# An mLSTM cell and a feed-forward on one core: cell steps visited in pairs, masks issued ahead

## Chip, core and metric

One core of a Trainium2 chip runs the whole kernel. The metric is the device time of one execution in microseconds (us), the median of the runs shown. Engines: PE is TensorE (PEld its weight loads), DVE VectorE, ACT ScalarE, POOL GpSimd, SP the engine that issues nearly all DMAs here.

## The reference, cut to what matters

Per batch row and head an mLSTM recurrence over 768 tokens; the result, laid out as 3072 tokens of 320, goes through a feed-forward of width 2048 with a leaky ReLU.

```python
# q, k, v, o_gate: (4, 8, 768, 40); i_gate, f_gate: (4, 8, 768)
for t in range(S):
    m_new = max(f[t] + m, i[t])
    f_stab, i_stab = exp(f[t] + m - m_new), exp(i[t] - m_new)
    m = m_new
    C = f_stab * C + i_stab * outer(v[t], k[t])          # 40 x 40 per head
    n = f_stab * n + i_stab * k[t]
    y[t] = sigmoid(o[t]) * (C @ q[t]) / max(abs(n . q[t]), 1)
x = y.transpose(0, 2, 1, 3).reshape(3072, 320)
h = x @ w_in                                             # 320 x 2048
out = maximum(0.01 * h, h) @ w_out                       # 2048 x 320
```

## The kernel before

The 768 tokens are cut into six chunks of 128 (c = 0 to 5). A **step** s is one chunk of one batch row, s = 4c + b, with all eight heads; there are 24. A step is computed in two halves of 64 tokens (u = 0, 1): scores inside a half, and a carried state of 40 x 42 per head that is advanced at each half's end.

The feed-forward runs one chunk behind the cell. In stage c, for c = 2 to 5, TensorE does the feed-forward of chunk c - 1 in 32 units, `ff_units(c - 1)`: units 0 to 15 are eight `pair`s of hidden tiles (`first` with three of the five contraction slots, `second` with the other two and the leaky ReLU on ScalarE), units 16 to 31 are the sixteen `part`s of the output, four for each batch row. Between units, in an order written out by hand, stand the cell's **visits** for chunk c, listed by `cell_units(c)`:

- `u_parts(s)`: scores and the two halves' state increments, into two PSUM banks `sd0`, `sd1` (64x64 tiles of TensorE, L595 and L600); then DVE multiplies the scores by the decays `w` into `qn` (L605) and adds the first increment to the state (`state_add`, L577).
- `u_mix(s)`: the output product, `pT` (L676); POOL advances the state (`state_next`, L573); DVE turns `pT` into blocks `hb` (L683), forms the denominators and the gated value in `xb` (L687), POOL divides (L690), DVE adds the second increment, which frees `sd1`, and turns `xb` back into `x` (L694); SP stores it to DRAM (`x_dr`, L697).
- `u_gates(c + 1)`: the gates of the next chunk turned to token order, `tg` (L312, L317), and copied out by DVE (L322, L324).

Stage 1 has `u_plain` in place of `u_mix`, and `u_x`, which transposes on TensorE. There the weights' conversion from 64-bit words still runs on DVE and ACT, dripped between the units (`now`).

What a step needs ahead of its visit is issued by `ahead(s)` (L814): the exponentials `prep_exp` (eight on ACT, L439, over `w` in place), `prep_kq` (two transposes and two multiplications on DVE, L486, L492), the loads of k, q and the decays `ea` for step s + 2, POOL's `state_next(s, 0)` and `prep_vu` (L459), and `prep_mask(s + 1)`, which adds the causal mask to the next step's `w` on POOL (L431). In stages 2 to 5 `ahead(s + 1)` follows `u_parts(s)`; in stage 1 it follows `u_plain(s)`, but for the last step. The exponentials lie in `lazy` and are issued three a unit from then on, ahead of the unit's own work; what is left is flushed in `u_parts`.

`gather_x` (L711) brings the stored `x` of a step into `xT`, the feed-forward's input, once unit 15 of the stage is through. After a mix, `load_late` loads the step-after-next's output gate, and `feed(s + 4)` loads k, v and `w` of the same row in the next chunk. The buffers that matter: `kqT`, `ea`, `vu`, `x` and `rb` (k, q, o as blocks) twice, `w` four times, `hb`, `xb` and `xT` once; PSUM has a pool `psc` of four banks for the cell and a pool `psf` of four for the feed-forward (`ph`, `po`). The orders on PE, DVE, ACT and POOL are those of the program text; SP's order is chosen by the scheduler.

Where the visits stand is one line (L957); with nine visits and 32 units they follow units 2, 5, 7, 10, 13, 15, 18, 21 and 23, one at a time:

```python
upto = sum(p <= i for p in place) if c == 1 else min(n_c, (i + 1) * n_c // (n_ff - 8))
```

Of the kernel before, what the change touches and what calls it, by code (L numbers as in the profile page):

```python
# [18 lines left out]
def kernel(  # L19
# [27 lines left out]
    B, H, S, D = q.shape  # L47
    P = 128
    BH = B * H
    NB = S // P  # L50
    NS = B * NB
# [86 lines left out]
    def subs(s):  # L138

        for u in range(2):  # L140
            yield u, ts(u, SL), slice(SL * (1 - u), SL * (1 - u) + D)
# [78 lines left out]
    def narrow_weights(n):  # L220

        if not wide:
            return
        raw, dst = raws.pop(n)
        words = raw.bitcast(U32).rearrange("p (c two) -> p c two", two=2)
        lo, hi = words[:, :, 0], words[:, :, 1]
        d = dst.bitcast(U32)
        low, top = lo.bitcast(F32), hi.bitcast(F32)  # L230
        nc.scalar.activation(dst, top, AF.Abs)
        yield
        nc.vector.tensor_scalar(
            dst, dst, scalar1=2.0**-15, scalar2=122879.9921875, op0=ALU.max, op1=ALU.min,
        )
        yield
        nc.vector.tensor_scalar(
            d, d, scalar1=0x07FFFFFF, scalar2=3, op0=ALU.bitwise_and, op1=ALU.logical_shift_left,
        )
        yield  # L240
        nc.vector.scalar_tensor_tensor(d, in0=hi, scalar=0xC0000000, in1=d, op0=ALU.bitwise_and, op1=ALU.bitwise_or)  # L241
        yield
        nc.vector.tensor_scalar(hi, d, scalar1=0xFF800000, scalar2=None, op0=ALU.bitwise_and)  # L243
        yield
        nc.vector.scalar_tensor_tensor(low, in0=lo, scalar=2.0**-52, in1=top, op0=ALU.mult, op1=ALU.mult)  # L245
        yield
        nc.vector.tensor_tensor(dst, dst, low, op=ALU.add)  # L247
# [108 lines left out]
    def natural(s, i):  # L356

        t = rb_t[s % NR][:, i]
        return t[:, : H * D].rearrange("p (h d) -> p h d", d=D)
# [67 lines left out]
                )  # L427

    def prep_mask(s):
        w = st[s]["w"]  # L430
        nc.gpsimd.tensor_tensor(w, w, cm2.unsqueeze(1).to_broadcast([P, H, SL]), op=ALU.add)  # L431

    def prep_exp(s):

        c, b = divmod(s, B)
        w = st[s]["w"]
        for h in range(H):
            bh = b * H + h
            yield nc.scalar.activation(w[:, h, :], w[:, h, :], AF.Exp, bias=gT[c][:, 0, bh : bh + 1], scale=1.0)  # L439
# [23 lines left out]
    def prep_qs(s):  # L463

        c, b = divmod(s, B)
        d = st[s]
        d["qs"] = wk.tile([P, Dm], F32, name="y")[:].rearrange("p (h d) -> p h d", d=D)
        nc.gpsimd.tensor_tensor(
            d["qs"], natural(s, 1), gT[c][:, 2, ts(b, H)].unsqueeze(2).to_broadcast([P, H, D]), op=ALU.mult,
        )  # L470
# [10 lines left out]
    def prep_kq(s):  # L481

        d = st[s]
        d["kqT"] = wk.tile([P, 2, PR * P], F32, name="kqT")
        for i in range(2):
            nc.vector.transpose(  # L486
                d["kqT"][:, i].rearrange("p (h t n) -> p h n t", n=TS, t=QW),
                raw_blocks(s, i, QW).rearrange("p (h n) d -> p h n d", n=TS),
            )
        for r in range(2):  # L490
            rows = ts(r, SL)
            nc.vector.tensor_tensor(  # L492
                mixed(s)[rows, 1 - r], d["kqT"][rows, 1].rearrange("p (h t) -> p h t", t=SL), d["ea"][rows], op=ALU.mult,
            )
# [10 lines left out]
    def u_split(s):  # L505

        d = st[s]
        d["kqT"] = wk.tile([P, 2, PR * P], F32, name="kqT")
        src = (d["k"], natural(s, 1))
        bank = [psc.tile([P, H, SL], F32, name=f"tk{r}", tag="c") for r in range(2)]  # L510
        for h in range(H):
            for i in range(2):
                for u, toks, rows in subs(s):
                    out_rows = rows if i == 0 else slice(SL * u, SL * u + D)
                    nc.tensor.matmul(
                        bank[u][out_rows, h, :], lhsT=src[i][toks, h, :D], rhs=ident[toks, toks], start=True, stop=True,
                    )
        for i in range(2):
            for u, toks, rows in subs(s):
                out_rows = rows if i == 0 else slice(SL * u, SL * u + D)  # L520
                nc.scalar.copy(d["kqT"][rows, i].rearrange("p (h t) -> p h t", t=SL), bank[u][out_rows])
# [275 lines left out]
        gates_T(c, bus.pop(c)[0])  # L797

    def cell_units(c):
        units = [(fn, c * B + n) for n in range(B) for fn in (u_parts, u_mix if c > 1 else u_plain)]  # L800
        if c + 1 < NB:
            units.insert(2 * B - 2, (u_gates, c + 1))
        if c == 1:
            units += [(u_x, s) for s in range(B, 2 * B)]
        return units

    lazy = {}

    def run(steps, n=None):

        for _ in range(H if n is None else n):
            next(steps, None)

    def ahead(s):  # L814

        if s < NS:
            if s < 2 * B:
                u_split(s)
            lazy[s] = prep_exp(s)
            if s < 2 * B:  # L820
                prep_qs(s)
            else:
                prep_kq(s)
            if s + NR < NS:
                load_late(s + NR, 0)
                load_late(s + NR, 1)
                if s + NR >= 2 * B:
                    spread_q(s + NR)
            state_next(s, 0)
            prep_vu(s)  # L830
            if s + 1 < NS:
                prep_mask(s + 1)

    def feed(s):
        load(s)
        spread(s)
# [78 lines left out]
    with tc.manual_schedule(engines={E.PE, E.DVE, E.Activation, E.Pool}):  # L915
        ffs = first_chunk()
        for s in (B, B + 1):
            feed(s)
            for i in range(1, 3):
                load_late(s, i)  # L920
            if s == B:
                load_weights(3)
        for n in range(3):
            load_weights(QN + n)
        for s in (B + 2, B + 3):
            feed(s)


        ffs = ffs[2:]
        fetch = {4: (3, 4), 8: (5, 6), 15: (7,)}  # L930
        place = (2, 5, 7, 10, 12, 15, 16, 18, 21, 22, 24, 26, 28)
        now = (None for n in range(2, QN + NF // 2) for _ in narrow_weights(n))
        for c in range(1, NB + 1):
            if c > 1:
                ffs = ff_units(c - 1)
            cells = cell_units(c) if c < NB else []
            n_ff, n_c = len(ffs), len(cells)
            done = fed = 0
            waiting = []
            for i in range(n_ff):  # L940
                if c == 1:
                    run(now, 2 if i < 10 else 3 if i < 14 else 4)
                    for n in fetch.get(i, ()):
                        load_weights(QN + n)
                    if i == 0:
                        prep_mask(B)
                        ahead(B)
                        load_fi(3)
                for steps in lazy.values():
                    run(steps, 3)  # L950
                ffs[i]()
                if c + 1 < NB:
                    if i == (1 if c == 1 else 0):
                        gates(c + 1)
                    if i == (3 if c == 1 else 2):
                        gates_exp(c + 1)
                upto = sum(p <= i for p in place) if c == 1 else min(n_c, (i + 1) * n_c // (n_ff - 8))  # L957
                while done < upto:
                    fn, s = cells[done]
                    fn(s)  # L960
                    done += 1
                    if fn is u_mix:
                        waiting.append(s)
                    if fn in ((u_mix, u_plain) if s < 2 * B - 1 else (u_parts,)):
                        ahead(s + 1)
                if i >= n_ff // 2 - 1:
                    for s in waiting:
                        gather_x(s)
                    waiting.clear()
                while fed < done:  # L970
                    fn, s = cells[fed]
                    fed += 1
                    if fn in (u_mix, u_plain):
                        load_late(s + NR, 2)
                        if s + NL < NS:
                            feed(s + NL)
# [31 lines left out]
```

## Time and profile before

| | |
|---|---|
| runs | 533.64, 534.17, 535.91 us; median 534.17 |
| profiled execution | 533.48 us, its span 531.7, mean granted clock 0.98 |
| PE, PEld busy | 517.3, 334.5 us of the span |
| DVE, ACT, POOL busy | 241.1, 168.0, 111.1 us |
| chunk boundaries on PE | 139.6, 219.6, 299.7, 379.8, 459.2 us |

A row of the profile says how often an instruction ran and how long one took; L12 is line 12 of the kernel. A busy PE is no sign of work at full speed[...]. A matmul in float32 leaves two records. "Idle before" is the engine's idle time ahead of an instruction, with what ended it; "issue" means that nothing in the profile did. A DMA's row on SP is its issue.

### The profile page before, as it was taken

The page shows a single profiled execution, that of the slowest core. Times are in us where ns is not written, and L with a number is a line of the kernel's source. Part 1 is how long each engine was busy: PE and PEld are TensorE (multiplying, and loading weights), DVE is VectorE, ACT ScalarE, POOL GpSimd, SP SyncE. Part 2 cuts the span into 40 slices and gives each one's busy share as a digit, 9 for nine tenths or more (in the row PEclk, how much of TensorE's full clock was granted, in tenths as well). Part 3 has the DMA queues.
Part 4 walks back from the last instruction along what each step waited for, and adds up shares of the span by engine and source line. Part 5 has one row for each costly group of instructions (what it writes and reads, how often), then busy time and mean ns, then how long its engine had stood idle before and what let it go on. Part 6 is the DMA issues. An engine that isn't in the chain of part 4 may idle for free.

```text
span 531.7 us, 11350 instructions
## 1 busy us (share of the span) xinstructions
PE 517.3 (97%) x4501; PEld 334.5 (63%) x4501; DVE 241.1 (45%) x431; ACT 168.0 (32%) x458; POOL 111.1 (21%) x145
## 2 busy tenths in 40 slices
PE   7879989999999999999999999999999999999997
PEld 7767878667545577545577555577555577544675
DVE  4788998999055526055616055614054432000000
ACT  4566767515434311134311134311134300122100
POOL 4245254153022223022223012323011100000000
PEclk9768999999999999999999999999999999999999
DMA  9977677878745647555547555546531221000000
GB/s 116 161 205 161 146 185 183 185 143 175 157 92 114 125 121 162 120 119 112 125 132 146 131 114 102 130 136 151 123 73 39 66 71 43 32 1 0 14 12 25
DMA packets 165284, 59.13 MB, mean 111 GB/s; under 512 B 128816, under 2 KB 156016, under 8 KB 165232
## 3 DMA queue, kind: packets, MB, share of 16 engines
q1 hardware_dynamic: 164848, 58.28, 50.2%
q8 instruction: 35, 0.57, 0.4%
q10 hardware_dynamic: 384, 0.13, 0.1%
q14 instruction: 17, 0.14, 0.1%
HBM read 51.68 MB, written 6.70 MB: 110 GB/s over the span
## 4 chain that ended last, share of the span: by engine, by line
PE 81%; DVE 7%; SPq 6%; DMA 2%; ACT 2%; issue 1%; POOL 1%; ACTq 0%; DVEq 0%; POOLq 0%
PE po L775 36%; PE ph L740 36%; PE pT L676 3%; SPq L213 3%; PE sd L595 3%; SPq L338 2%; DVE raw L245 1%; SPq L352 1%; PE sd L600 1%; DVE qn L605 1%; DVE w_out L247 1%; DMA rb<-in_q_dram 1%; DVE w_out L241 1%; DVE raw L243 1%; DMA raw<-in_moe_w_in_dram 1%
## 5 line engine op out<-in xcount | busy, mean ns | idle before, releaser
L740 PE MATMUL ph<-xT,w_in 64*128 64x512 f32 (+1 forms) x1120 | 217.3, 538 | 0.6 <-ACT acts L748 0.6
L775 PE MATMUL po<-w_out,acts 128*128 128x320 f32 x768 | 213.3, 435 | 0.0
L775 PEld LDWEIGHTS po<-w_out,acts 128*128 128x128 f32 x768 | 143.8, 190 | 59.7 <-issue 1.8
L740 PEld LDWEIGHTS ph<-xT,w_in 64*128 64x128 f32 x1120 | 107.1, 189 | 91.1 <-issue 84.4
L748 ACT ACTIVATE acts<-ph 128x512 f32<-128x512 f32 (+1 forms) x112 | 53.9, 534 | 145.6 <-PE ph L740 145.5
L605 DVE TENSOR_TENSOR qn<-w,sd 64x512 f32<-64x512 f32 x40 | 27.4, 686 | 125.6 <-PE sd L600 90.1
L573 POOL TENSOR_TENSOR S<-S,f 40x336 f32<-40x336 f32 x36 | 30.7, 854 | 187.8 <-PE pT L676 146.8
L439 ACT ACTIVATE w<-w,gT 128x64 f32<-128x64 f32 (+1 forms) x192 | 52.5, 351 | 1.0 <-DVE w L425 1.0
L783 ACT COPY y<-po 128x320 f32<-128x320 f32 x12 | 5.1, 426 | 86.6 <-PE po L775 86.6
L783 ACT COPY hn<-po 128x320 f32<-128x320 f32 x12 | 5.1, 427 | 86.3 <-PE po L775 86.3
L690 POOL TENSOR_TENSOR xb<-xb,den 128x320 f32<-128x320 f32 x16 | 11.7, 729 | 88.9 <-DVE xb L687 88.9
L431 POOL TENSOR_TENSOR w<-w,i 128x512 f32<-128x512 f32 x20 | 26.7, 1333 | 10.2 <-DMA w<-a_dr 10.1
L683 DVE STREAM_TRANSPOSE hb<-pT 128x512 f32<-128x512 f32 x16 | 11.5, 717 | 38.1 <-PE pT L676 38.1
L595 PEld LDWEIGHTS sd<-kqT 40*64 40x64 f32 x640 | 20.3, 135 | 10.8 <-issue 9.3
L595 PE MATMUL sd<-kqT 40*64 40x64 f32 x640 | 23.0, 221 | 0.0
L492 DVE TENSOR_TENSOR qn<-kqT,ea 64x512 f32<-64x512 f32 x32 | 22.4, 701 | 1.1
L676 PEld LDWEIGHTS pT<-qn,S 128*64 128x64 f32 x512 | 16.2, 138 | 10.5 <-issue 6.9
L600 PE MATMUL sd<-S,vu 64*40 64x42 f32 x576 | 20.6, 215 | 0.7 <-POOL vu L459 0.7
L694 DVE STREAM_TRANSPOSE x<-xb 128x512 f32<-128x512 f32 x16 | 17.6, 1102 | 8.0 <-POOL xb L690 8.0
L486 DVE STREAM_TRANSPOSE kqT<-rb 128x512 f32<-128x512 f32 x32 | 20.7, 682 | 0.0
L600 PEld LDWEIGHTS sd<-S,vu 64*40 64x40 f32 x576 | 18.2, 111 | 0.8 <-POOL vu L459 0.8
L577 DVE TENSOR_TENSOR S<-S,sd 40x336 f32<-40x336 f32 x36 | 18.1, 503 | 0.9
(126 smaller groups left out, 369.1 us busy)
## 6 DMA issues: line engine op xcount, KB each, us to landing
w<-a_dr SPq DMA_DIRECT2D x40, 128.0 KB
rb<-in_k_dram SPq DMA_DIRECT2D x64, 80.0 KB
rb<-in_q_dram SPq DMA_DIRECT2D x64, 80.0 KB
rb<-in_o_gate_dram SPq DMA_DIRECT2D x64, 80.0 KB
ea<-a_dr SPq DMA_DIRECT2D x32, 128.0 KB
kn<-in_k_dram SPq DMA_DIRECT2D x24, 160.0 KB
raw<-in_moe_w_out_dram SPq DMA_DIRECT2D x6, 640.0 KB
S<-in_v_dram SPq DMA_DIRECT2D x80, 40.0 KB
```

The lines of the kernel that those rows point to most:

```text
L431: nc.gpsimd.tensor_tensor(w, w, cm2.unsqueeze(1).to_broadcast([P, H, SL]), op=ALU.add)
L439: yield nc.scalar.activation(w[:, h, :], w[:, h, :], AF.Exp, bias=gT[c][:, 0, bh : bh + 1], scale=1.0)
L486: nc.vector.transpose(d["kqT"][:, i].rearrange("p (h t n) -> p h n t", n=TS, t=QW), raw_blocks(s, i, QW).rearrange("p (h n) d -> p h n d", ...
L492: nc.vector.tensor_tensor(mixed(s)[rows, 1 - r], d["kqT"][rows, 1].rearrange("p (h t) -> p h t", t=SL), d["ea"][rows], op=ALU.mult,)
L573: nc.gpsimd.tensor_tensor(new, old, g, op=ALU.mult)
L595: nc.tensor.matmul(bank[1 - u][toks, h, :], lhsT=kqT[rows, 0, ts(h, SL)], rhs=kqT[rows, 1, ts(h, SL)], start=True, stop=True,)
L600: nc.tensor.matmul(dC[u][:, h].rearrange("p k d -> p (k d)"), lhsT=d["ku"][toks, h], rhs=S_v[s % NL][toks, u, h, :, :V1], start=True, stop ...
L605: nc.vector.tensor_tensor(mixed(s)[toks, u], w[toks], bank[1 - u][toks], op=ALU.mult)
L676: nc.tensor.matmul(pT[DP * r : DP * (r + 1), j * P + u * SL : j * P + (u + 1) * SL], lhsT=S[:, u, h, :], rhs=m[:, u, h, :], start=True, st ...
L740: nc.tensor.matmul(ph[r][:, cols], lhsT=w_row(r, slot, j), rhs=xT[DP * r : DP * (r + 1), slot, cols], start=(slot == 0), stop=(slot == KC ...
L748: nc.scalar.activation(acts[:, f, cols], ph[r][:, cols], AF.Prelu, alpha=0.01)
L775: nc.tensor.matmul(po[n][:], lhsT=acts[:, f, ts(n, P)], rhs=w_out[:, f, :], start=(f == 0), stop=(f == NF - 1),)
```

## The change

In stages 2 to 5 the visits of two steps stand together: `u_parts` of both after unit 2, `u_mix` of both after unit 6, `u_parts` of the other two after unit 14, and after unit 19 `u_gates` and their two `u_mix`. `ahead(s + 2)` now follows `u_mix(s)`. The exponentials of a step wait three units before they start. The masks are issued on POOL at unit 0 (steps 2 and 3 of the chunk) and at unit 12 (the first two of the next chunk), and at the end of stage 1 for step 9; `masked` keeps a mask from being added twice. In stage 1 the order of the visits stays, and `ahead(9)` follows `u_plain(7)`.

```diff
     def prep_mask(s):
+        if s in masked:
+            return
+        masked.add(s)
         w = st[s]["w"]
...
     def cell_units(c):
-        units = [(fn, c * B + n) for n in range(B) for fn in (u_parts, u_mix if c > 1 else u_plain)]
+        if c == 1:
+            units = [(fn, c * B + n) for n in range(B) for fn in (u_parts, u_plain)]
+            units.insert(2 * B - 2, (u_gates, c + 1))
+            return units + [(u_x, s) for s in range(B, 2 * B)]
+        units = [(fn, c * B + n + m) for n in range(0, B, 2) for fn in (u_parts, u_mix) for m in range(2)]
         if c + 1 < NB:
             units.insert(2 * B - 2, (u_gates, c + 1))
-        if c == 1:
-            units += [(u_x, s) for s in range(B, 2 * B)]
         return units
...
     def ahead(s):
...
+            if s >= 2 * B:
+                late[s] = 3
             lazy[s] = prep_exp(s)
...
-            if s + 1 < NS:
+            if s + 1 <= 2 * B:
                 prep_mask(s + 1)
...
+        late = {}
+        masks = {0: (2, 3), 12: (4, 5)}
+        pairs = (2, 2, 6, 6, 14, 14, 19, 19, 19)
...
-                for steps in lazy.values():
-                    run(steps, 3)
+                for s, steps in lazy.items():
+                    if s in late and late[s] > 0:
+                        late[s] -= 1
+                    else:
+                        run(steps, 3)
+                for n in masks.get(i, ()) if 1 < c < NB else ():
+                    if c * B + n < NS:
+                        prep_mask(c * B + n)
                 ffs[i]()
...
-                upto = sum(p <= i for p in place) if c == 1 else min(n_c, (i + 1) * n_c // (n_ff - 8))
+                upto = min(n_c, sum(p <= i for p in (place if c == 1 else pairs)))
                 while done < upto:
...
-                    if fn in ((u_mix, u_plain) if s < 2 * B - 1 else (u_parts,)):
+                    if fn is u_plain and s < 2 * B - 1 or fn is u_parts and s == 2 * B - 1:
                         ahead(s + 1)
+                    elif fn is u_mix:
+                        ahead(s + 2)
+                    elif fn is u_plain:
+                        prep_mask(s + 2)
+                        ahead(s + 2)
```

More of the change, by code (lines that the diff above doesn't have):

```diff
@@ L799, in cell_units @@
     def cell_units(c):
-        units = [(fn, c * B + n) for n in range(B) for fn in (u_parts, u_mix if c > 1 else u_plain)]
+        if c == 1:
[3 more added lines that the diff above has]
+        units = [(fn, c * B + n + m) for n in range(0, B, 2) for fn in (u_parts, u_mix) for m in range(2)]
         if c + 1 < NB:
             units.insert(2 * B - 2, (u_gates, c + 1))
-        if c == 1:
-            units += [(u_x, s) for s in range(B, 2 * B)]
         return units
+    masked = set()
     lazy = {}
```

## The prediction

> **What bounds the kernel now.** I read the page first (busy shares, chain), then busy time by chunk, then the timeline of the weight loads around one visit, then the DMA queue's timeline. The page (busy time; the chain by engine):
>
> ```profile
> PE 517.3 (97%) x4501; PEld 334.5 (63%) x4501; DVE 241.1 (45%) x431; ACT 168.0 (32%) x458; POOL 111.1 (21%) x145
> ...
> PE 81%; DVE 7%; SPq 6%; DMA 2%; ACT 2%; issue 1%; POOL 1%; ACTq 0%; DVEq 0%; POOLq 0%
> ```
>
> TensorE bounds it, and where it does not (the first 45 us, and chunk 1, where VectorE converts weights) the change does nothing much. By chunk (start:end, length, busy of each engine; chunk 3, chunk 5, the closing feed-forward):
>
> ```profile
> core 0: us, PE busy (x) PEld busy (x) DVE busy (x) ACT busy (x) POOL busy (x), PEclk, DMA share, GB/s
> 219.60:299.70 80.10, 80.10 (x679) 47.71 (x678) 34.50 (x64) 20.28 (x60) 17.05 (x20) 1.00 0.59 129
> 379.80:459.20 79.40, 79.40 (x609) 47.06 (x608) 26.75 (x48) 17.50 (x48) 7.12 (x9) 1.00 0.24 61
> 459.20:531.70 72.50, 69.30 (x289) 39.65 (x288) 0.00 (x0) 10.81 (x21) 0.00 (x0) 1.00 0.03 12
> ```
>
> In chunks 2 to 5 TensorE is busy without a gap at full clock; no other engine passes 44%. So only TensorE's own time counts there, unless a new wait appears. The chain shows the feed-forward alone, in the last stage:
>
> ```profile
> 459.31 34.53 PE ph L740 x160
> 493.85 34.66 PE po L775 x128
> ```
>
> That is 69.19 us. Chunk 3 does the same 288 records in 80.10, so its four `u_parts`, four `u_mix` and one `u_gates` cost 10.9. What one visit costs, from TensorE's weight loads (start, length, count, idle before):
>
> ```profile
> 225.72 0.19 PEld L740 LDWEIGHTS ph<-xT,w_in 64*128 64x128 f32 x2 [0.24 <-issue]
> 226.67 0.14 PEld L595 LDWEIGHTS sd<-kqT 40*64 40x64 f32 x2 [0.76 <-issue]
> ...
> 227.75 0.30 PEld L740 LDWEIGHTS ph<-xT,w_in 64*128 64x128 f32 x4
> 228.28 0.19 PEld L740 LDWEIGHTS ph<-xT,w_in 64*128 64x128 f32 x2 [0.23 <-issue]
> 228.72 0.19 PEld L740 LDWEIGHTS ph<-xT,w_in 64*128 64x128 f32 x2 [0.24 <-issue]
> ...
> 233.96 1.01 PEld L676 LDWEIGHTS pT<-qn,S 128*64 128x64 f32 x32 [0.76 <-issue]
> ```
>
> Undisturbed, pairs of loads stand 0.43 us apart (0.19 + 0.24). From 225.72 to 228.72 there are four pairs, 1.72 us undisturbed, but 3.00 pass: the visit costs 1.28. Inside a visit the records repeat evenly: the 32 `pT` loads take 1.01, less the last load's 0.14, over 15 steps: 0.058 a step; 16 steps are 0.93. So **0.35 us of each visit is entering and leaving**: the weights of the first matmul behind a switch are not loaded under the matmul before (idle 0.76 instead of 0.24), and the same on the way back.
>
> [...] `ph` runs as 64x128 tiles, `sd` as 64x64, `pT` as 128x64, `po` as 128x128, and a visit shows two switches of some 0.17 us each (0.35/2). [...] Here the last gather's issue ends at 296.46 and the matmul that reads it starts at 299.71 without a wait, so its landing is hidden, by an unknown part of 3.2 us.
>
> **The change, part by part.**
>
> *Joined visits (the gain).* Per chunk 2 to 4, nine visits become four: parts+parts after i=2, mix+mix after i=6, parts+parts after i=14, gates+mix+mix after i=19. Chunk 5: eight become four. Sixteen joins of equal mode (4 per chunk) save two switches each, 16 x 0.35 = 5.6. Three joins of gates to mix still change mode once, so about one switch: 3 x 0.17 = 0.5. Together 6.1. How well a second step follows the first is not in the trace: at best without loss (0)[...]. I take 0.04, as inside `ph` a pair that waits for ScalarE keeps the 0.43 rhythm: 16 x 0.04 = 0.6. **Gain 5.5** (bounds 3.4 to 6.1). No instruction is added; the numbers of matmuls, VectorE, GpSimd and DMA instructions stay, only places change.
>
> *PSUM.* Two `u_parts` hold all four psc banks; `sd1` of each is free only after its own `u_mix`. In the compiled order the two `pT` of the first pair take the two `sd0` banks (free after `state_add` of i=2, VectorE done about 4 us before). In the second pair `tg` takes one `sd0`, `pT` the other, and the last `pT` takes `tg`'s, freed by the L324 copy. In chunk 3 `tg` ended near 269.0 and that copy ended about 269.5; the first `pT` keeps TensorE busy until about 0.95 after `tg`. Cost 0; if VectorE were late there, a few tenths, three times.
>
> *VectorE.* Two mixes and two `ahead` in a row: `hb` to `x` is 155.05 to 158.95, 3.9 us, `prep_kq` 2.7 (149.67 to 152.42), so 13.2 us from i=6. With units of 2.57 (first), 1.72 (second) and 2.15 (`part`) and joined visits of 2.2, i=6 ends at 17.6 us of the chunk and the next parts start at 37.0: done by 32, 5 us to spare. Parts at 6.9 take VectorE 3.8 (4 x 0.69 + 2 x 0.50) after 9.1: 13 before 17.6. Cost 0.
>
> *Masks (POOL).* 1.33 us each (L431), the same number, now at i=0 and i=12. A mask waits for its `w` DMA; behind it on POOL stands `state_next` of the mix at 17.6 us. *Exponentials* start three units later, six a unit at 0.25 to 0.35 us: some 5 us of ScalarE in about 6.5 beside 2 to 3 us of relus; a relu may come 2 us late, and the four psf banks give a pair of 4.3 us. Cost 0. *Chunk 1:* `ahead(9)` comes after `u_plain(7)`, 2.7 us of VectorE at about 130, where it falls idle from 134 to 148. Cost 0, give or take 0.5.
>
> *SP and the chunk's end* (what is late next). A joined mix lets its DMAs out together. The queue before, at a chunk's end (start, length, what):
>
> ```profile
> 260.87 2.01 SPq L382 DMA_DIRECT2D rb<-in_k_dram  x4
> 262.98 1.87 SPq L382 DMA_DIRECT2D rb<-in_q_dram  x4
> 264.95 1.10 SPq L405 DMA_DIRECT2D ea<-a_dr  x2
> ...
> 290.52 1.56 SPq L697 DMA_DIRECT2D x_dr<-x  x4
> ...
> 293.90 2.56 SPq L711 DMA_DIRECT2D xT<-x_dr  x4
> ```
>
> After: `pT` of the third step ends near 51.4 us of the chunk, `x` is ready 4.0 later, 55.4. Ahead of the last gathers in the compiled order stand, twice, x_dr, k, q, ea: 2 x (1.56 + 2.01 + 1.87 + 1.10 + 0.4 of gaps) = 13.9, then eight gathers at 0.67: 5.4. Issued at 74.7, landed perhaps 1.5 later, 76.2. The next chunk starts at 78.3 to 78.7. Slack about 2 us; cost 0. What follows on SP (o, kn, v and w of two steps, 22 issues, 12.5 us) ends near 9 us of the next chunk, so the i=0 masks are done before 13: POOL's `state_next` has 4 us to spare.
>
> **Sum:** 533.48 (profiled; span 531.7) - 5.5 = 528.0. The median of the runs is 0.69 above the profiled one: **528.7**.
>
> **Rivals.** (1) *Joins nearly not free*[...]; 16 x 0.18 + 0.5 = 3.4, and a chunk-end wait of 0.5 us four times takes 2: gain 1.4, 532.8, no change. For it: each join brings new waits; against: `ph` pairs with waits lose nothing. (2) **Slower: the gathers come late.** The 36 issues from `x_dr` to the last gather are back to back; k and q bring 80 KB in 0.49 us, about 163 GB/s, as much as the busiest of the page's 40 slices in chunks 2 to 5 moved (162), and one such group took 3.17 instead of 2.0 (283.45). Past the 2 us of slack each microsecond counts four times: 1.4 us late cancels the gain, 2.1 us makes it slower by over 0.5%. At 3.5 late: 528.7 + 14 = 542.7. Against it: now it also ends close (296.46 for 299.71) and holds. (3) *The change doesn't do what it says*: a bank, mask or exponential makes TensorE wait inside a joined visit, 3 us (VectorE's chain after `pT`) at up to eight mixes, 552; the compiled bank order speaks against it.
>
> **Chances.** Forecast (gain over 2.7, the bound of 0.5%, about what a measurement of this kernel tells from no change) 0.73; rival 1 and small chunk-end waits, within 0.5%, 0.14; rival 2 0.10 and rival 3 0.03, slower, 0.13. Low end: gain 6.1 plus 0.5 of chunk 1 and 0.6 for the runs' spread, 527.0. High end: rival 1's 532.8 and a few tenths of gathers late, 534.0; beyond lie rivals 2 and 3. The forecast's own range is 527.0 to 531.5.
>
> **What would show it.** Right: chunks 2 to 4 of about 78.7 us, chunk 5 78.2, `pT` in runs of 64 records over about 2.0 us, no idle TensorE; `ph` of the next chunk not released by a DMA. Wrong: an idle of TensorE ahead of `pT` ended by VectorE (bank), ahead of `ph` ended by xT's DMA (rival 2), relus held by exponentials, or a gap of 0.2 us between two `sd` or `pT` runs (rival 1).

## The result, and the profile after

The changed kernel takes **528.66 us** in the median of six runs (528.14 to 530.43); the kernel before took 534.22 on the same chip (533.18 to 535.91). The ratio is 0.9896, 95% interval 0.9876 to 0.9915: **faster by 1.0%**, where 528.7 was forecast. The profiled execution took 528.25 us, its span 526.4.

The page of the changed kernel, busy time and the chain by engine:

```profile
PE 513.2 (97%) x4501; PEld 336.3 (64%) x4501; DVE 240.3 (46%) x431; ACT 168.1 (32%) x458; POOL 113.0 (21%) x145
...
PE 83%; SPq 6%; DVE 4%; DMA 2%; ACT 2%; issue 1%; POOL 1%; ACTq 0%; POOLq 0%
```

The numbers of instructions are those of before, and TensorE bounds it as before. By chunk (chunk 3, chunk 5, the closing feed-forward; start:end, length, busy time of each engine):

```profile
core 0: us, PE busy (x) PEld busy (x) DVE busy (x) ACT busy (x) POOL busy (x), PEclk, DMA share, GB/s
218.46:297.23 78.77, 78.77 (x680) 47.77 (x680) 34.30 (x64) 20.29 (x60) 17.35 (x20) 1.00 0.58 128
375.99:454.03 78.04, 78.04 (x611) 47.09 (x610) 23.73 (x44) 15.62 (x40) 8.41 (x10) 1.00 0.26 64
454.03:526.40 72.37, 69.19 (x289) 39.57 (x288) 0.00 (x0) 10.81 (x21) 0.00 (x0) 0.99 0.03 12
```

TensorE is still busy without a gap, at full clock. Chunks 2 to 5 take 78.82, 78.77, 78.77 and 78.04 us; before they took 80.11, 80.11, 80.11 and 79.42. That is 314.39 for 319.75, **5.36 us less**. All the rest of the span is 212.0 us in both. A joined visit on the weight loads of TensorE (start, length, idle before):

```profile
235.30 0.19 PEld L743 LDWEIGHTS ph<-xT,w_in 64*128 64x128 f32 x2 [0.23 <-issue]
236.25 1.95 PEld L679 LDWEIGHTS pT<-qn,S 128*64 128x64 f32 x64 [0.76 <-issue]
238.26 0.30 PEld L743 LDWEIGHTS ph<-xT,w_in 64*128 64x128 f32 x4
238.80 0.19 PEld L743 LDWEIGHTS ph<-xT,w_in 64*128 64x128 f32 x2 [0.24 <-issue]
239.23 0.19 PEld L743 LDWEIGHTS ph<-xT,w_in 64*128 64x128 f32 x2 [0.24 <-issue]
```

From 235.30 to 239.23 stand four pairs of `ph` again, 1.72 us undisturbed, and 3.93 pass: two `pT` cost 2.21 us, against 2 x 1.28 apart (a single `pT`, at 233.96 in the kernel before, costs 1.29 by the same count). The 64 loads are one even run: (1.95 - 0.14)/31 = 0.058 a step, the rhythm of a single visit, so the joint itself costs nothing. The chain of waits, last stage:

```profile
454.03 34.53 PE ph L743 x160
488.56 34.66 PE po L778 x128
```

It is the closing feed-forward, 69.19 us as before, two records for each of its 80 and 64 matmuls. The end of chunk 3 on SP, whose next `ph` begins at 297.23:

```profile
274.23 1.46 SPq L700 DMA_DIRECT2D x_dr<-x  x4
275.78 2.82 SPq L382 DMA_DIRECT2D rb<-in_k_dram  x4
...
281.87 1.66 SPq L700 DMA_DIRECT2D x_dr<-x  x4
...
288.63 5.16 SPq L714 DMA_DIRECT2D xT<-x_dr  x8
```

One group of k took 2.82 us instead of 1.8 to 2.0, and the last gather is issued by 293.79, 3.4 us ahead of `ph`. By the DMA records of the trace its data were moved by 295.07 and its landing was signalled by 295.61, 1.28 and 1.82 us behind the issue.

### The profile page after: what moved, and what is told of

It reads as the page before. It is cut to its first block, busy times and chain, and to the rows that moved or that the text cites. A ratio compares the mean times of both kernels' runs of the same rounds, so it can differ in the third digit from the quotient of the medians.

```text
span 526.4 us, 11333 instructions
## 1 busy us (share of the span) xinstructions
PE 513.2 (97%) x4501; PEld 336.3 (64%) x4501; DVE 240.3 (46%) x431; ACT 168.1 (32%) x458; POOL 113.0 (21%) x145
## 4 chain that ended last, share of the span: by engine, by line
PE 83%; SPq 6%; DVE 4%; DMA 2%; ACT 2%; issue 1%; POOL 1%; ACTq 0%; POOLq 0%
PE po L778 38%; PE ph L743 36%; PE pT L679 3%; SPq L213 3%; PE sd L598 3%; SPq L338 2%; SPq L352 1%; PE sd L603 1%; DMA rb<-in_q_dram 1%; DVE raw L245 1%; DVE qn L608 1%; DMA S<-in_v_dram 0%; DMA raw<-in_moe_w_in_dram 0%; PE tk L518 0%; PE hN L649 0%
## 5 line engine op out<-in xcount | busy, mean ns | idle before, releaser
L778 PE MATMUL po<-w_out,acts 128*128 128x320 f32 x768 | 211.1, 434 | 0.0
L442 ACT ACTIVATE w<-w,gT 128x64 f32<-128x64 f32 (+1 forms) x192 | 51.1, 348 | 3.1 <-POOL w L434 2.1
L434 POOL TENSOR_TENSOR w<-w,i 128x512 f32<-128x512 f32 x20 | 28.1, 1411 | 104.7 <-ACT bu L294 53.0
L495 DVE TENSOR_TENSOR qn<-kqT,ea 64x512 f32<-64x512 f32 x32 | 27.3, 854 | 0.9
L598 PE MATMUL sd<-kqT 40*64 40x64 f32 x640 | 21.5, 220 | 0.0
```

The lines of the kernel that those rows point to most:

```text
L495: nc.vector.tensor_tensor(mixed(s)[rows, 1 - r], d["kqT"][rows, 1].rearrange("p (h t) -> p h t", t=SL), d["ea"][rows], op=ALU.mult,)
L598: nc.tensor.matmul(bank[1 - u][toks, h, :], lhsT=kqT[rows, 0, ts(h, SL)], rhs=kqT[rows, 1, ts(h, SL)], start=True, stop=True,)
L778: nc.tensor.matmul(po[n][:], lhsT=acts[:, f, ts(n, P)], rhs=w_out[:, f, :], start=(f == 0), stop=(f == NF - 1),)
```

## Experiments

Each run changes the changed kernel in one respect, but for one that starts from the kernel before and one that repeats the changed kernel. "Stages" means chunks 2 to 5 on TensorE: where one kernel was profiled twice, a stage differed by no more than 0.05 us, while the rest of the span went from 210.3 to 213.5 us over the profiled executions here. Where a difference is small, I go by the stages.

### Is it the joining? Two ways to take the visits apart

First with the last visits at 16, 18 and 20:

```diff
-        pairs = (2, 2, 6, 6, 14, 14, 19, 19, 19)
+        pairs = (2, 3, 6, 7, 13, 14, 16, 18, 20)
```

> The changed kernel with its visits taken apart again: pairs = (2, 3, 6, 7, 13, 14, 16, 18, 20), so the order of the visits, ahead, the masks and the late exponentials stay, but no two visits stand together. If the gain is TensorE's switches between tile shapes, all 19 joins are undone: chunks 2 to 4 back at about 80.1 us, chunk 5 at 79.4, total 534 (ratio 1.00 to before). If the earlier masks or the other order of the cell's work brought it, it stays near 528.7 (0.99).

Measured: 542.98 us, ratio 1.0158 (1.0130 to 1.0185). In the total neither: a new wait had come. SP's timeline and TensorE's, at the end of chunk 2 and of chunk 3:

```profile
201.42 2.56 SPq L714 DMA_DIRECT2D xT<-x_dr  x4
204.08 1.97 SPq L382 DMA_DIRECT2D rb<-in_o_gate_dram  x4
206.14 0.39 SPq L340 DMA_DIRECT2D kn<-in_k_dram  x1
206.63 2.66 SPq L343 DMA_DIRECT2D S<-in_v_dram  x4
209.34 1.26 SPq L397 DMA_DIRECT2D w<-a_dr  x2
...
211.32 1.57 SPq L700 DMA_DIRECT2D x_dr<-x  x4
...
218.68 2.56 SPq L714 DMA_DIRECT2D xT<-x_dr  x4
```

```profile
221.86 2.14 PE L743 MATMUL ph<-xT,w_in 64*128 64x512 f32 x4 [1.99 <-issue]
305.90 2.52 PE L743 MATMUL ph<-xT,w_in 64*128 64x512 f32 x8 [1.46 <-ACT hn L786]
```

The last `x` was ready on DVE at 201.6 us, but SP stored it only at 211.32: the loads fed by the mix just before stood ahead of it, without a gap. The last gather was issued up to 221.24 and `ph` began 0.6 us later, after a wait. The rows name "issue" and a copy of ScalarE, and SP's rows show what was late; at the third border the same wait, 1.1 us, is put down to xT's DMA. So the total tells nothing of the joins, and is the prediction's rival of late gathers, brought about by separating two mixes. Only chunk 2, ahead of the first wait, is undisturbed: from its first `ph` to the end of its `po` it takes 80.38 us, against 78.89 in the changed kernel, 1.5 us more with all its visits apart. The second split leaves room between the mixes:

```diff
-        pairs = (2, 2, 6, 6, 14, 14, 19, 19, 19)
+        pairs = (2, 3, 6, 7, 13, 14, 14, 16, 19)
```

> The changed kernel with its four joined visits of a chunk taken apart again, places (2, 3, 6, 7, 13, 14, 14, 16, 19): same order of the work, same masks and exponentials, the gates' transposes stay joined to a visit, and the last two mixes stand three pieces apart, so that SyncE's list of loads between them is through before the last gathers. Theory (the gain is the entering and leaving of visits): a joined pair of parts costs 2.26 us on TensorE against 2 x 1.28 apart, a joined pair of mixes 2.22 against 2 x 1.28, so 2 x 0.30 + 2 x 0.35 = 1.30 us a chunk come back, 5.2 us over four: 533.9 us, and each of chunks 2 to 5 about 1.3 us longer. Rival (the gain is the order of the steps and the masks handed out early, the joining is not needed): 528.7 us, chunks as in the changed kernel. If the gathers are late again as they were in the first split, TensorE waits at the chunks' starts and the time is above 536 us.

Measured: **533.40 us**, ratio 0.9984 (0.9973 to 0.9995), chunks 80.11, 80.11, 80.11, 79.23, no wait of TensorE in them. Chunk 3, in the columns of the table by chunk:

```profile
219.41:299.52 80.11, 80.11 (x681) 47.70 (x680) 34.19 (x64) 20.28 (x60) 17.34 (x20) 1.00 0.57 127
```

With the order of the steps, the early masks and the held exponentials all kept, 5.2 us of the stages' 5.36 go with the joints alone. The rival (order and masks) falls. The gates stay joined here, to the parts at 14; chunk 5 has no gates, so its third mix stands there, and that chunk is 0.2 shorter than before.

### What a join saves: per change of tile shape, and where

The kernel before, with the mix of one step and the parts of the next put together, which are unlike tiles:

```diff
-                upto = sum(p <= i for p in place) if c == 1 else min(n_c, (i + 1) * n_c // (n_ff - 8))
+                upto = min(n_c, sum(p <= i for p in (place if c == 1 else (2, 6, 6, 11, 11, 17, 17, 17, 22)
+                    if c + 1 < NB else (2, 6, 6, 11, 11, 17, 17, 22))))
```

> The kernel before, its order, ahead and masks untouched, but u_mix(s) and u_parts(s + 1) stand together (with u_gates between the third pair): 9 visits become 5, chunk 5 has 5 for 8. Inside a joined visit the tile shape still changes (128x64 to 64x64). If each change of tile shape costs 0.17 us, 4 of 18 changes go in chunks 2 to 4 and 3 of 16 in chunk 5: 15 x 0.17 = 2.6 us, chunk 3 at 79.4, total 531.6. If each visit costs 0.35 whatever its shape, 15 visits go: 5.2 us, chunk 3 at 78.7, total 529. If joins bring new waits, it is slower than that.

Measured: 533.41 us, ratio 0.9985 (0.9975 to 0.9996); stages 318.52, so 1.2 us gained, less than either theory expected. On the weight loads `pT` and `sd` together cost 2.36 us against 2.56 apart: 0.20 saved, for one change of shape avoided of four, while like tiles save 0.35 and avoid two. "Per visit" falls. What both theories had missed is the place. The kernel before has its third `pT` exactly where `ph` ends and `po` begins (first fence); the changed kernel has that border bare (second):

```profile
259.59 0.19 PEld L740 LDWEIGHTS ph<-xT,w_in 64*128 64x128 f32 x2 [0.24 <-issue]
260.54 1.01 PEld L676 LDWEIGHTS pT<-qn,S 128*64 128x64 f32 x32 [0.76 <-DVE qn L492]
261.62 1.10 PEld L775 LDWEIGHTS po<-w_out,acts 128*128 128x128 f32 x5
```

```profile
258.66 0.19 PEld L743 LDWEIGHTS ph<-xT,w_in 64*128 64x128 f32 x2 [0.24 <-issue]
259.61 2.18 PEld L778 LDWEIGHTS po<-w_out,acts 128*128 128x128 f32 x9 [0.76 <-issue]
```

The border shows the same idle of 0.76 with or without a visit: by these rows its change of shape is paid in any case, and a visit there pays one change less. Both the changed kernel and this one moved the visit away and pay the border again, 0.20 us a chunk. With it, a chunk here should save 2 x 0.20 + 0.08 (`pT`, `tg` and `sd` together: 3.36 for 3.44) - 0.20 = 0.28, and 0.28 was measured in chunks 2 and 4 (80.11 to 79.83). Chunk 3 gained only 0.08: ahead of its first visit one pair of `ph`'s loads took 0.40 instead of 0.19, and 0.2 was lost there. Chunk 5 has no gates, and had no visit on the border before: 3 x 0.20 expected, 0.60 measured (79.42 to 78.82). Why the group of three saves 0.08 only stays open. Two runs put visits on borders:

```diff
-        pairs = (2, 2, 6, 6, 14, 14, 19, 19, 19)
+        pairs = (2, 2, 6, 6, 15, 15, 19, 19, 19)
```

> The changed kernel with the second pair of u_parts after unit 15 in place of 14: at the border from ph (64x128 tiles) to po (128x128), where the shape changes anyway. The number of visits stays. If a change of shape is what costs, one of them goes in each of four chunks: 4 x 0.17 = 0.7 us, chunks 2 to 4 at 78.6, total 528.0. If a visit costs by itself (waits, first weights), nothing changes: 528.7.

Measured: 527.65 us, ratio 0.9887 (0.9866 to 0.9907); chunks 78.61, 78.57, 78.57 and 77.84, each 0.20 shorter than in the changed kernel, 0.8 in all. The other also puts the first parts between two chunks:

```diff
-        pairs = (2, 2, 6, 6, 14, 14, 19, 19, 19)
+        pairs = (-1, -1, 6, 6, 15, 15, 19, 19, 19)
...
+            while 1 < c < NB and done < sum(p < 0 for p in pairs):
+                fn, s = cells[done]
+                fn(s)
+                done += 1
```

> As e5_edge, and the first pair of u_parts moved ahead of unit 0, to the border from po to ph. If a change of shape costs 0.17 us, two of them go in each of four chunks: 1.4 us, chunks 2 to 4 at 78.4, total 527.3. If a visit costs by itself, 528.7. If the first pair is not ready so early (kqT, qn or exponentials late), TensorE waits ahead of sd at the chunk's start and it is slower.

Measured: 528.59 us, ratio 0.9891 (0.9874 to 0.9908). A miss in the total. From the end of stage 1 (141.1 us here, 139.6 in the changed kernel) to the end it took 385.5 us against 386.8, 1.3 less, close to the 1.4 expected. What hid it in this execution lies ahead of the stages, where the two kernels are the same: the granted clock was halved for one stretch of 3.4 us in stage 1, and TensorE fell 1.3 us behind the changed kernel in it. The same stretch in this run and in the changed kernel, PE busy throughout in both, with 57 and 81 records:

```profile
77.90:81.30 3.40, 3.40 (x57) 2.85 (x50) 2.22 (x5) 0.42 (x2) 1.28 (x1) 0.50 0.63 133
77.90:81.30 3.40, 3.40 (x81) 3.09 (x73) 2.63 (x6) 0.76 (x4) 1.27 (x1) 1.00 0.66 92
```

Then the changed kernel and the version with the border, both on one chip:

> The changed kernel as it is, beside the next one on the same chip, so that a difference of less than a microsecond between the two can be told: 528.7 us.

> The changed kernel with the second pair of parts one piece later, at piece 15, where ph ends and po begins (as in the run before of that name). Theory (a visit on that border is one change of tile shape cheaper, and the changed kernel gave up what the kernel before had there): 0.20 us a chunk, 0.8 us less than the changed kernel on the same chip, 527.9 us. Rival (the 1 us between the two seen on different chips was between the chips or between executions' first 100 us): no difference, 528.7 us.

Measured: 527.28 us (ratio 0.9869, 0.9849 to 0.9890) and 527.23 us (0.9864, 0.9843 to 0.9885). The stages differ as expected, 314.44 and 313.62, but the rest of the two profiled spans is 211.1 and 211.6. So 0.8 us is there in the trace and cannot be told in the time, and the same kernel gave 528.66 and 527.28 on two chips.

### Are the early masks and the held exponentials needed?

Neither (each mask goes to POOL at the end of the visit, directly ahead of its exponentials, which start at once):

```diff
     def ahead(s):
...
-            if s >= 2 * B:
-                late[s] = 3
+            if s > 2 * B:
+                prep_mask(s)
...
-        masks = {0: (2, 3), 12: (4, 5)}
+        masks = {}
...
-                        prep_mask(s + 2)
```

> The changed kernel without the masks handed out ahead and without the exponentials held back by three pieces: each mask product goes to GpSimd directly ahead of its step's exponentials, at the end of the visit that makes room for it. Theory of the prediction (masks and exponentials are hidden either way): 528.7 us, no new wait of TensorE. Rival: a mask product stands on GpSimd behind the state and gate products of the same visit, the exponentials wait for it some 4 to 5 us at the head of ScalarE's queue, the relu behind them is late, and TensorE waits for a bank, 1 to 3 us at each of two visits a chunk: 536 to 550 us.

Measured: **562.79 us**, ratio 1.0534 (1.0501 to 1.0566), worse than the rival's range. One wait in each of the four stages, ahead of `ph`, 22.0 us in all. Waits of the engines, then one visit in the timelines of POOL, ACT and PE:

```profile
PE ph L743 <- ACT acts L751: 22.0, 4, 5.6
```

```profile
254.78 0.72 POOL L693 TENSOR_TENSOR xb<-xb,den 128x320 f32<-128x320 f32 x1 [2.60 <-DMA rb<-in_k_dram]
255.47 1.27 POOL L434 TENSOR_TENSOR w<-w,i 128x512 f32<-128x512 f32 x1
```

```profile
256.77 0.83 ACT L442 ACTIVATE w<-w,gT 128x64 f32<-128x64 f32 x3 [6.54 <-POOL w L434]
257.50 1.06 ACT L751 ACTIVATE acts<-ph 128x512 f32<-128x512 f32 x2
```

```profile
258.13 2.92 PE L743 MATMUL ph<-xT,w_in 64*128 64x512 f32 x5 [5.64 <-ACT acts L751]
```

`pT` began at 244.19. The second step's mask (255.47) stands on POOL behind the second mix's division (254.78), which waits for DVE to do the first step's chain, its kq and then the second's (the row names a DMA, but DVE ends the gated value that is divided at 254.64). Its exponentials wait 6.54 us at the head of ACT's queue; the relu at 257.50 stands behind them, the four psf banks wait for the relus, and TensorE waits 5.64. The stages lost 33.1 us, 11.1 more than the waits. Granted clock (PEclk, third from the end, columns as in the table by chunk) in stretches after the same wait:

```profile
252.00:258.10 6.10, 0.49 (x4) 0.00 (x0) 5.54 (x11) 1.33 (x5) 3.34 (x5) 0.90 0.67 152
258.10:262.00 3.90, 3.87 (x9) 3.27 (x11) 1.51 (x2) 3.80 (x13) 0.28 (x1) 0.50 0.67 157
262.00:266.00 4.00, 4.00 (x17) 3.27 (x16) 0.00 (x0) 0.51 (x2) 0.00 (x0) 0.78 0.63 169
266.00:270.00 4.00, 4.00 (x21) 3.49 (x19) 0.00 (x0) 0.79 (x3) 0.00 (x0) 1.00 0.58 123
```

Half clock for 3.9 us and 0.78 for 4.0 lose 1.95 + 0.88 = 2.8 us of work; four times that would be 11.3. Then each device alone. Only the early masks:

```diff
-            if s >= 2 * B:
-                late[s] = 3
```

> The changed kernel with the masks handed out at pieces 0 and 12 as they are, but the exponentials not held back: a step's exponentials may start at the piece after the visit that makes room for it. Theory (what the run without both devices lost is ScalarE's wait for the second step's mask, which stood behind the second mix's products of VectorE and GpSimd; with the masks done before the visit no exponential waits, whether held back or not): 528.7 us, no wait of TensorE at ph. Rival (it is the holding back that keeps ScalarE free for the relus): as without both, 555 to 563 us, with waits of ph for acts.

Measured: 530.48 us, ratio 0.9923 (0.9894 to 0.9952). Stages 78.81, 78.82, 78.78, 78.04: those of the changed kernel, no wait in them. But at the end of stage 1, step 9's exponentials, no longer held, wait for their mask at the head of ACT's queue, with the last steps' copies into `xT` behind them:

```profile
132.31 0.83 ACT L442 ACTIVATE w<-w,gT 128x64 f32<-128x64 f32 x3 [7.63 <-POOL w L434]
133.04 0.35 ACT L729 COPY xT<-xt 128x256 f32<-128x256 f32 x1
```

In the changed kernel the wait in this place is 2.11 us. Here `ph` of chunk 2 waits 0.75 us for the last of the copies, and 1.4 us in the run without both devices; in the two runs that hold the exponentials back it does not wait. In this execution the clock was also halved from 76.6 to 80.0 us, as in the run with two borders. The median's 1.8 us more than in the changed kernel, on another chip, is not split further. Only the holding back:

```diff
     def ahead(s):
...
+            if s > 2 * B:
+                prep_mask(s)
...
-        masks = {0: (2, 3), 12: (4, 5)}
+        masks = {}
...
-                        prep_mask(s + 2)
```

> The changed kernel with the exponentials held back by three pieces as they are, but each mask handed to GpSimd at the end of the visit, directly ahead of its step's exponentials. Theory: the second step's mask is done 12.6 us after the pair of mixes begins on TensorE (as without both devices); with three pieces of 2.15 us between, its exponentials reach ScalarE about 8 us after that beginning and wait some 3 to 4 us, less than the two pairs of banks cover, so 528.7 to 532 us. Rival (the early masks are what is needed, holding back does nothing): 550 to 563 us.

Measured: 528.15 us, ratio 0.9867 (0.9832 to 0.9902), stages 314.43, no wait of TensorE in them, though ACT still waits:

```profile
ACT w L442 <- POOL w L434: 45.0, 11, 6.6
```

So the rival falls here too: in chunks 2 to 5 either device is enough, and one must be there. At the end of stage 1 only the holding back spares `ph` a wait.

### How much room have the gathers?

```diff
-        pairs = (2, 2, 6, 6, 14, 14, 19, 19, 19)
+        pairs = (2, 2, 6, 6, 14, 14, 20, 20, 20)
```

> The changed kernel with its last visit (gates and two mixes) one piece later, at piece 20: 2.15 us later on TensorE. Theory (the last gathers of a chunk land 1.9 us before the next chunk's first matmul: issued by 75.4 us of a chunk of 78.8 us, landed some 1.5 us later): 0 to 0.5 us a chunk at three borders, 528.7 to 530.2 us. Rival (there is no such limit, or it is much wider): 528.7 us here and at piece 22 too.

Measured: 528.00 us, ratio 0.9881 (0.9851 to 0.9911). Chunks 78.81, 79.67, 78.77, 78.04: one border of three lost 0.85, at the start of chunk 3, for 0 to 0.5 expected at each. There the last gather was issued by 218.49 and `ph` began at 218.86; at the next border, issued by 296.27 and begun at 298.53, nothing was lost. So the room is used up at piece 20. And at 22 (the same line with 22):

> The changed kernel with its last visit at piece 22, 6.46 us later on TensorE than in the changed kernel. Theory of the slack of about 1.9 us: the gathers come 6.5 - 1.9 = 4.6 us late at three borders between chunks (the last chunk of visits issues fewer loads and has more room): 13.7 us more, 542.4 us, with a wait of ph for xT's DMA at the starts of the chunks. Rival (the last visit may stand anywhere, its transfers are hidden): 528.7 us.

Measured: **542.10 us**, ratio 1.0148 (1.0120 to 1.0176), 13.4 more than the changed kernel, for 13.7 expected. The wait at the first border, by TensorE's timeline:

```profile
222.37 9.52 PE L743 MATMUL ph<-xT,w_in 64*128 64x512 f32 x32 [3.89 <-DMA xT<-x_dr]
```

The waits at the three borders are 3.89, 2.20 and 2.32 us, 8.4 of the stages' 13.3; the rest follows them. At the first border the 32 records take 9.52 instead of the 7.07 us of an undisturbed start of a chunk, in part at half clock (the last section). At the other two they take 1.2 and 1.1 us too long at full clock, more than half of it within the first five records. So the total came as expected, but not as three equal delays of 4.6 us: that it agrees so closely is luck.

## Why the prediction was right, point by point

- **Bound, and what shows it.** Right: only TensorE's own time in chunks 2 to 5 moved. Forecast lengths were 78.7 and 78.2 us; they are 78.8 and 78.0.
- **0.35 us for entering and leaving.** Right. By the second split and the weight loads, a joined pair of mixes saves 0.35 of 2.56, a pair of parts 0.30 or 0.35.
- **0.04 for a joint.** On the safe side: none between mixes, 0.05 at four of the eight joints of parts, some 0.2 in all for the 0.6 assumed.
- **Gates joined to a mix, 0.17 each.** 0.20: `tg` and two `pT` cost 2.90 us, apart 0.88 + 2 x 1.28.
- **What the sum left out: what the change takes away.** The sum put this at nothing, but the visit on the border of `ph` and `po` was lost, 3 x 0.20 us. In chunk 3, 0.35 + 0.30 + 0.35 + 0.55 for the gates' group - 0.20 = 1.35 us, measured 1.34, forecast 1.41; chunk 5, which had no visit on that border, gave 1.38, forecast 1.24. This error and the joints' nearly cancel: 5.36 for 5.5. That the median came within 0.04 us is luck: the same kernel gave 527.28 on another chip.
- **"Twice 0.17 a visit".** The mixed pair (0.20 for one change of shape fewer), the like pair (0.30 to 0.35 for two) and the border (0.20 for one) put a change at 0.15 to 0.20 us here. The group of three (0.08 for two fewer) does not fit this size. What goes on in TensorE at a change was not shown, beyond the idle of the weight loads: 0.76 us ahead of a visit and at the bare border, 0.24 inside `ph`.
- **PSUM, VectorE.** Cost 0, right: no wait inside a joined visit; the pair of mixes is through on DVE 33.4 us into the chunk (251.84) for 32 forecast, and the next parts begin at 37.2.
- **Masks and exponentials, cost 0.** Right for the kernel as changed, wrong in what it rests on. The second mask waited for its `w` and began 12.9 us into chunk 3, done at 14.1 for "before 13", 4.5 us ahead of `state_next`. But I named the four psf banks as the cover of a late relu and left a mask or exponential to rival 3 (0.03), without seeing that a place for the masks decides: with neither device it is 34 us slower.
- **Gathers.** Right: x ready at 55.8 us of the chunk for 55.4, issued by 75.3 for 74.7. The 1.5 us for the landing was an estimate. By the DMA records of the trace of before, the data of the last gather were moved 1.45 to 1.56 us behind its issue, and in the changed kernel 1.28 to 1.50; its landing was signalled 1.82 to 1.98 us behind in the changed kernel, 1.2, 1.6 and 2.5 us ahead of the starts of chunks 3, 4 and 5 (218.46, 297.23 and 375.99), for a slack of about 2. The moves by 2.15 and 6.46 us show the edge close to where it was put. But a delay counts at three borders, not four: at the end of chunk 5 the run at piece 22 has no wait. Rival 2 is real: it decided both the first split and the run at piece 22. It did not come true in the change itself because the edge is one piece away.
- **Chunk 1 within 0.5 us.** Not decided: the time outside the stages scatters by more, in part with the clock (the last section).

## What to carry to other kernels

Here small matmuls of another tile shape cut into a long uniform stream on a bound TensorE, and with the same number of instructions the time followed the changes of shape, the group of three apart: 5.2 us of the stages for visits put side by side with their like, 0.8 for a visit placed where the stream changes shape anyway. Where a kernel looks like this one, count those changes and measure what one is worth. Before joining, follow the second step's inputs through the program's order on each engine: what one step issued between the two visits is now behind both or between them. In the run without both devices a mask that came late held ScalarE for 6.54 us and the relu behind it with it, and in the first split the length of SP's queue decided: `x`, ready at 201.6, was stored at 211.32. Then measure how far the last visit may move before its transfers are late, so that the place is chosen with a known margin.

## What was not expected of the hardware

Waits of TensorE cost half as much again as their own length in the run without both devices (33.1 us for 22.0), and the length alone did not say which would be followed by a slower clock. After waits of 3.89 us (piece 22) and 5.64 us (neither device) the granted clock stood at 0.50 for 3.41 and 6.83 us, and after waits of 1.46, 2.20 and 2.32 us it stayed at 1.00. But after the wait of 1.99 us in the first split it was halved too. The clock's changes in one trace lie whole steps of 3.41 us apart: in the run without both devices it was halved at 168.17, 256.91, 342.25 and 430.99 us, which are 26, 25 and 26 steps; in the traces of before and after, the stretches at one clock ahead of stage 1 last 3.41, 6.83, 10.24 and 13.65 us, 1 to 4 steps. The first split (wait of 1.99 us) and the run at piece 22 (wait of 2.20 us), cut along these steps (columns as in the table by chunk):

```profile
219.22:222.63 3.41, 1.42 (x6) 0.69 (x6) 0.00 (x0) 0.42 (x1) 0.00 (x0) 1.00 0.60 156
222.63:226.04 3.41, 3.41 (x10) 2.25 (x9) 0.00 (x0) 0.00 (x0) 0.00 (x0) 0.50 0.76 155
226.04:229.45 3.41, 3.41 (x18) 2.37 (x17) 0.00 (x0) 1.33 (x4) 0.00 (x0) 1.00 0.51 99
```

```profile
301.54:304.95 3.41, 2.05 (x8) 1.14 (x6) 0.00 (x0) 0.42 (x1) 0.00 (x0) 1.00 0.55 155
304.95:308.37 3.42, 2.41 (x8) 1.07 (x10) 0.00 (x0) 0.00 (x0) 0.00 (x0) 1.00 0.54 144
```

The wait of 1.99 us lies within one step, in which TensorE is busy for 1.42 of 3.41 us, and the next step runs at half clock. The wait of 2.20 us lies across two, and neither is followed by half clock. Near 74 us, in stage 1, five of the fourteen traces have a step in which TensorE is idle for 0.48 of its length: four were followed by half clock and one was not. In the other nine, idle for at most 0.44 of a step there, none was (before: busy for 1.94 us of the step from 73.88 to 77.29; after: 1.97 of that from 74.92 to 78.33; the clock 1.00 in the step behind both). Where the steps lie differs between executions: the first half clock starts at 12.44 us in the trace of before and at 13.48 in that of after. I take this as why like waits cost differently here, and as part of the scatter outside the stages (1.3 us in the run with two borders).

A step that was busy for 1.42 of 3.41 us (the first split) was followed by half clock, and near 74 us four that were busy for about half of their length. What decides it these runs do not show.
